# Low-rank mix in plain float32 with V in four bands, and ScalarE copying the second head's transposed exponents in every attention step

## The chip, the cores and the metric

The kernel runs on one core of one Trainium2 chip. The metric is the device time of one execution in microseconds (us). TensorE is called PE, VectorE DVE, ScalarE ACT, GpSimd POOL in the rows; PEld is PE's weight load, SP the engine that issues most DMAs.

## The reference

Three stages follow each other on 2 batches of 768 tokens with 512 features. Everything is float32.

```python
# 1. attention, 8 heads of 64, a window of 96 keys and 8 global keys, ALiBi bias
a = softmax(scale * q @ k.T + bias, masked);  x = a @ v
# 2. low-rank mix over the tokens (rank 32), then a feed-forward network
h = x.transpose(0, 2, 1) @ U @ V              # U [768, 32], V [32, 768]
u = x + h.transpose(0, 2, 1)
x = u + np.maximum(u @ w_ch1, 0.0) @ w_ch2    # 512 -> 2048 -> 512
# 3. real part of a 2-D FFT, normalisation, a second feed-forward network
```

The change is in the low-rank mix between the attention and the first feed-forward network, and in one copy of the attention.

## The kernel before

**Numbers.** The fast matmuls take operands in a rounded form of float32 (`fp32r`, FR in the code). To keep precision the kernel splits a matrix into a rounded part and a remainder (names `wh`/`wo`, `xh`/`xl`, `gh`/`gl`, `vh`/`vl`): ACT casts, then POOL or DVE subtracts, and PE multiplies the parts one after the other. Attention and transposes use plain float32, one matmul per product; such a matmul stands as two records in the trace.

**Attention.** `attn` goes through 8 head pairs `c`, each in 3 steps `j`. In a step PE makes scores (line 484), DVE adds the bias and finds the maximum (492), ACT takes exponents (504), PE transposes them (515) into a `ps_h` bank for each of the two heads `z`, and an engine copies the bank to SBUF as `pt`: ACT at line 517, DVE at line 519. Before the feed-forward network runs (`side_mode` False) the first head always goes to DVE, and the second to ACT for `j` 0 and 1, to DVE for `j` 2. PE then multiplies with V's rows (535), ACT copies (539), and after three steps PE transposes (550) and DVE scales into `xall` (558).

**Low-rank mix.** For each batch `lr_sum` adds U^T x over six token tiles. `us` holds U's rounded part and remainder, each twice, as 128 columns; for every tile and half of the features ACT casts `xh` (337), `xl` is subtracted (338; DVE for batch 0, POOL for batch 1), and PE makes two matmuls of 256 columns (339, 340). Then ACT and DVE make `R` out of the sum (349, 350), and for each tile PE multiplies it with `vh` and `vl` (356, 357), DVE adds into `xall` (358), and some tiles are transposed for the feed-forward network (270, ACT 272, DVE 273).

**Feed-forward.** `ffn` goes through 16 chunks `c` of the hidden size for each block of 512 tokens. In iteration `c` PE makes h(c), 12 matmuls of 512 columns at line 203, and then a(c-1), 12 matmuls at line 225; I use these names below. For chunk `c` ACT casts `wh` (179) and POOL subtracts `wo` in two halves (182); h(c) needs the first half from its third matmul on. In the first block the weights arrive as int64-packed doubles and are decoded two iterations ahead: ACT line 164, DVE lines 166, 168, 170 in that order, the last writing `w`. `wh` and `wo` have three buffers each, so `wh`(c) cannot start before a(c-3) is done.

**Order.** A generator of side work (`drive`) gives one piece after each quarter of an iteration: first the rest of the attention, then batch 1's low-rank mix with the transposes of tiles 6 and 7, then those of tiles 4 and 5. A scheduler sets the final order on each engine; each engine works through its own queue in order. The first block begins at 100.9 us, and batch 1's mix at 158.9 us. PSUM has two `ps_sd` banks; during the first block the attention, `lr_sum` and the transposes of batch 1 share them.

Of the kernel before, what the change touches and what calls it, by code (L numbers as in the profile page):

```python
# [35 lines left out]
class Prog:  # L36
# [252 lines left out]
    def lr_setup(self, pool):  # L289
        nc = self.nc  # L290
        t0, t2, u64, v64 = self.lrt
        ur = t0[:, 2 * NT * RK:]
        for z in range(4):
            self.decode(ur, u64, z)
        yield
        uraw = ur.rearrange("p (t r) -> p t r", t=NT)
        self.us = pool.tile([P, NT, 4 * RK], FR, name="us")
        self.vh = pool.tile([P, S], FR, name="vh")
        self.vl = pool.tile([P, S], FR, name="vl")
        nc.gpsimd.memset(self.vl[2 * RK:P, :].bitcast(F32), 0.0)  # L300
        us = self.us
        for c in (0, 2):
            h, l = us[:, :, c * RK:(c + 1) * RK], us[:, :, (c + 1) * RK:(c + 2) * RK]
            nc.scalar.copy(h, uraw)
            nc.gpsimd.tensor_tensor(l, uraw, h.bitcast(F32), ALU.subtract)
        yield

    def lr_setup2(self, pool):
        nc = self.nc
        t0, t2, u64, v64 = self.lrt  # L310
        vraw = t2[:, 0:S]
        for z in range(4):
            self.decode(vraw, v64, z)
            yield
        nc.scalar.copy(self.vh, vraw)
        nc.gpsimd.tensor_tensor(self.vl[0:2 * RK, :], vraw[0:2 * RK, :], self.vh[0:2 * RK, :].bitcast(F32), ALU.subtract)
        yield

    def w_first(self):
# [4 lines left out]
        self.w_split(0)  # L324
        yield

    def lr_sum(self, b, pool, half):
        nc = self.nc
        if half == 0:
            self.tps = self.psum("m")  # L330
        tps = self.tps
        c = slice(half * 256, half * 256 + 256)
        for t in range(NT):
            x = self.x[b * NT + t]
            xh = pool.tile([P, 256], FR, tag="xh", bufs=2, name=f"xh{b}{t}{half}")
            xl = pool.tile([P, 256], FR, tag="xl", bufs=2, name=f"xl{b}{t}{half}")
            nc.scalar.copy(xh, x[:, c])
            (nc.vector if b == 0 else nc.gpsimd).tensor_tensor(xl, x[:, c], xh.bitcast(F32), ALU.subtract)  # L338
            nc.tensor.matmul(tps[:, c], lhsT=self.us[:, t, :], rhs=xh, start=t == 0, stop=False)
            nc.tensor.matmul(tps[:, c], lhsT=self.us[:, t, :], rhs=xl, start=False, stop=t == NT - 1)  # L340
            yield

    def lr(self, b, pool, halves, tiles):
        nc = self.nc
        for h in halves:
            yield from self.lr_sum(b, pool, h)
        tps = self.tps
        R = pool.tile([P, D], FR, tag="R", bufs=1, name=f"R{b}")
        nc.scalar.copy(R, tps)
        nc.vector.tensor_tensor(R[64:128, :], tps[64:128, :], R[64:128, :].bitcast(F32), ALU.subtract)  # L350
        yield
        for t in range(NT):
            x = self.x[b * NT + t]
            s = slice(t * P, (t + 1) * P)
            hp = self.psum("m")
            nc.tensor.matmul(hp, lhsT=self.vh[:, s], rhs=R, start=True, stop=False)
            nc.tensor.matmul(hp, lhsT=self.vl[:, s], rhs=R, start=False, stop=True)
            nc.vector.tensor_tensor(x, hp, x, ALU.add)
            yield
# [89 lines left out]
    def attn(self, pool, lag1=1, lag2=2):  # L449
# [58 lines left out]
        def s3(u):  # L508
            c, j = U[u]
            pr = st[u]  # L510
            pt = [pool.tile([P, 512], F32, tag="pt", bufs=4, name=f"pt{c}{j}{z}") for z in range(2)]
            for z in range(2):
                tp = self.psum("tr")
                for i in range(4):
                    nc.tensor.transpose(tp[:, i * P:(i + 1) * P], pr[z][:, i * P:(i + 1) * P], self.ident)  # L515
                if self.side_mode or z == 1 and j < 2:
                    nc.scalar.copy(pt[z], tp)  # L517
                else:
                    nc.vector.tensor_copy(pt[z], tp)
            st[u] = pt  # L520
# [300 lines left out]
def arm(tc, pg, fast):  # L821
    with ExitStack() as ctx2:
# [4 lines left out]
        if fast:  # L827
# [14 lines left out]
            pg.w_load(2)  # L842
            while pg.heads < 4:
                step(att, 1)
            for _ in pg.lr_sum(0, pool, 0):
                step(att, 1)
            for _ in chain(pg.lr_setup2(pool), pg.w_first()):
                step(att, 1)
# [2 lines left out]
        else:  # L851
# [161 lines left out]
```

## Time and profile before

| | |
|---|---|
| median of 3 runs | 716.91 us (716.83 to 717.27) |
| the profiled execution | 717.96 us, of which the span of the instructions is 716.2 us |
| PE busy | 694.5 us, 97% of the span |
| DVE, ACT, POOL busy | 51%, 41%, 43% |
| mean granted PE clock | 0.986 |

A busy share is an average over stages. PE's is so high that the few places where PE waits, or runs at a lower granted clock, are what there is to look for; the page's second part, busy tenths in 40 slices, puts them at 60 to 70 us and 160 to 200 us.

### The profile page before, as it was taken

The page shows a single profiled execution, that of the slowest core. Times are in us where ns is not written, and L with a number is a line of the kernel's source. Part 1 is how long each engine was busy: PE and PEld are TensorE (multiplying, and loading weights), DVE is VectorE, ACT ScalarE, POOL GpSimd, SP SyncE. Part 2 cuts the span into 40 slices and gives each one's busy share as a digit, 9 for nine tenths or more (in the row PEclk, how much of TensorE's full clock was granted, in tenths as well). Part 3 has the DMA queues.
Part 4 walks back from the last instruction along what each step waited for, and adds up shares of the span by engine and source line. Part 5 has one row for each costly group of instructions (what it writes and reads, how often), then busy time and mean ns, then how long its engine had stood idle before and what let it go on. Part 6 is the DMA issues. An engine that isn't in the chain of part 4 may idle for free.

```text
span 716.2 us, 9707 instructions
## 1 busy us (share of the span) xinstructions
PE 694.5 (97%) x3584; PEld 569.0 (79%) x3584; DVE 362.4 (51%) x722; ACT 296.3 (41%) x551; POOL 307.5 (43%) x258
## 2 busy tenths in 40 slices
PE   9998999996899999999999999999999999999995
PEld 8776777775678888888888888888888888888884
DVE  4779797655386754348737888124832111211112
ACT  3776666644243444334433334222233333332320
POOL 3104103237456655545534574424454444454450
PEclk9999999998799999999999999999999999999999
DMA  8846618554548877666656442221233223332301
GB/s 258 294 169 208 226 65 256 176 175 149 169 135 298 266 247 255 233 238 211 232 196 213 147 177 89 88 83 66 74 118 133 88 89 113 121 120 97 108 31 64
DMA packets 34393, 115.93 MB, mean 162 GB/s; under 512 B 4128, under 2 KB 4640, under 8 KB 32032
## 3 DMA queue, kind: packets, MB, share of 16 engines
q1 hardware_dynamic: 33024, 111.63, 46.0%
q0 software_dynamic: 1312, 3.59, 1.6%
q8 instruction: 30, 0.49, 0.3%
q14 instruction: 27, 0.22, 0.1%
HBM read 95.27 MB, written 19.92 MB: 161 GB/s over the span
## 4 chain that ended last, share of the span: by engine, by line
PE 90%; DVE 3%; issue 2%; POOL 2%; ACT 1%; DMA 0%; SPq 0%; DVEq 0%; POOLq 0%; ACTq 0%
PE ps_acc L225 35%; PE ps_h L203 35%; PE ps_sd L535 4%; PE ps_acc L484 3%; PE ps_h L515 2%; PE wu L80 2%; PE ps_sd L270 1%; PE ps_sd L484 1%; PE ps_sd L732 1%; POOL wo L182 1%; POOL xl L338 1%; PE ps_sd L746 1%; PE ps_sd L515 1%; PE ps_sd L708 1%; PE ps_sd L759 1%
## 5 line engine op out<-in xcount | busy, mean ns | idle before, releaser
L182 POOL TENSOR_TENSOR wo<-w,wh 128x512 fp32r<-128x512 f32 x192 | 266.6, 1409 | 288.7 <-ACT wh L179 285.3
L203 PE MATMUL ps_h<-uT,wh 128*128 128x512 f32 x768 | 239.9, 393 | 0.0
L211 DVE SCALAR_TENSOR_TENSOR gl<-ps_h,gh 128x512 fp32r<-128x512 f32 x96 | 65.9, 686 | 226.8 <-ACT gh L210 226.7
L179 ACT CAST wh<-w 128x1024 fp32r<-128x1024 f32 x96 | 101.0, 1052 | 172.5 <-PE ps_acc L225 139.8
L203 PEld LDWEIGHTS ps_h<-uT,wh 128*128 128x128 f32 x768 | 141.5, 188 | 29.5 <-issue 2.0
L225 PE MATMUL ps_acc<-wh,gh 128*128 128x512 f32 x384 | 153.4, 400 | 0.0
L225 PE MATMUL ps_acc<-wo,gh 128*128 128x512 f32 x384 | 151.8, 395 | 0.0
L225 PE MATMUL ps_acc<-wh,gl 128*128 128x512 f32 x384 | 151.7, 395 | 0.0
L203 PE MATMUL ps_h<-uT,wo 128*128 128x512 f32 x384 | 150.0, 391 | 0.0
L210 ACT ACTIVATE gh<-ps_h 128x512 fp32r<-128x512 f32 x96 | 57.5, 599 | 148.1 <-PE ps_h L203 148.1
L225 PEld LDWEIGHTS ps_acc<-wh,gl 128*128 128x128 f32 x384 | 73.4, 191 | 15.8
L225 PEld LDWEIGHTS ps_acc<-wh,gh 128*128 128x128 f32 x384 | 73.5, 191 | 14.7 <-issue 0.7
L225 PEld LDWEIGHTS ps_acc<-wo,gh 128*128 128x128 f32 x384 | 73.5, 191 | 14.2
L203 PEld LDWEIGHTS ps_h<-uT,wo 128*128 128x128 f32 x384 | 72.1, 188 | 15.4
L168 DVE SCALAR_TENSOR_TENSOR wr<-wr 128x1024 int32<-128x1024 int32 x32 | 47.9, 1498 | 32.5 <-ACT wr L164 31.2
L504 ACT ACTIVATE T<-T,m 128x256 f32<-128x256 f32 (+1 forms) x96 | 47.8, 499 | 28.2 <-DVE m L492 27.9
L164 ACT ACTIVATE wr<-wr 128x1024 f32<-128x1024 f32 x32 | 36.7, 1147 | 0.0
L535 PE MATMUL ps_sd<-pt,vb 128*64 128x128 f32 x384 | 35.3, 287 | 0.4 <-ACT pt L517 0.4
L492 DVE CUSTOM_DVE_ANT_0 T<-ps_acc,dist 128x256 f32<-128x256 f32 (+1 forms) x76 | 28.4, 418 | 11.0 <-PE ps_acc L484 7.0
L535 PEld LDWEIGHTS ps_sd<-pt,vb 128*64 128x64 f32 x384 | 26.0, 139 | 8.2 <-issue 5.2
L170 DVE SCALAR_TENSOR_TENSOR w<-wr 128x1024 int32<-128x1024 int32 x16 | 24.8, 1548 | 0.6
L437 POOL TENSOR_SCALAR q<-q 128x768 f32<-128x768 f32 x4 | 4.4, 1097 | 47.7 <-PE ps_sd L535 22.9
(171 smaller groups left out, 626.5 us busy)
## 6 DMA issues: line engine op xcount, KB each, us to landing
w<-wscr SPq DMA_DIRECT2D x80, 512.0 KB, 3.3
wr<-wl SPq DMA_DIRECT2D x17, 1024.0 KB, 5.9
wr<-wl SPq DMA_DIRECT2D x60, 256.0 KB, 5.3
wscr<-w SPq DMA_DIRECT2D x16, 512.0 KB, 6.7
wscr<-wd SPq DMA_DIRECT2D x16, 512.0 KB, 2.8
vb<-vw SPq DMA_DIRECT2D x8, 768.0 KB, 5.9
k<-qkg SPq DMA_DIRECT2D x4, 704.0 KB, 7.2
out<-qkt SPq DMA_DIRECT2D x11, 256.0 KB, 3.3
```

Source lines behind the costliest of these rows:

```text
L164: nc.scalar.activation(hi.bitcast(F32), hi.bitcast(F32), AF.Copy, scale=2.0 ** -112))
L168: nc.vector.scalar_tensor_tensor(lo, hi, 3, lo, ALU.logical_shift_left, ALU.bitwise_or)
L179: nc.scalar.copy(hi, raw)
L182: nc.gpsimd.tensor_tensor(lo[:, h], raw[:, h], hi[:, h].bitcast(F32), ALU.subtract)
L203: nc.tensor.matmul(hp, lhsT=w[:, s], rhs=u[:, dd, :], start=n == 0, stop=n == 11)
L210: nc.scalar.activation(gh, hp, AF.Relu)
L211: nc.vector.scalar_tensor_tensor(gl, hp, 0.0, gh.bitcast(F32), ALU.max, ALU.subtract)
L225: nc.tensor.matmul(acc[t], lhsT=g[:, s], rhs=w[:, D:2 * D], start=pf == 0 and m == 0, stop=pf == NF - 1 and m == 2)
L484: nc.tensor.matmul(sp[z][:, o:o + n], lhsT=q[ROWS[z], ts], rhs=win(k[ROWS[z]], t), start=True, stop=True)
L492: nc.vector.tensor_tensor_reduce(out=T[z][:, s], in0=sp[z][:, s], in1=self.dist[z][:, dcol[t]:dcol[t] + width[t]], op0=ALU.add, op1=ALU.mi ...
L504: nc.scalar.activation(T[z][:, s], T[z][:, s], AF.Exp, bias=m[z][:, i:i + 1], scale=-1.0, accum_out=st["s", c, z][:, j, i:i + 1])
L535: nc.tensor.matmul(pv[y * HD:(y + 1) * HD, z * P:(z + 1) * P], lhsT=v[:, vc, d], rhs=pt[z][:, o:o + P], start=i == 0, stop=i == n - 1)
```

## The change

`us` becomes U itself, four times side by side, in plain float32, written by one POOL instruction. `lr_sum` takes x as it is: `xh`, `xl` and their casts and subtractions are gone, and one plain float32 matmul takes the place of two rounded ones. Batch 0 keeps its two halves of 256 columns; batch 1 does all 512 columns at once, in 6 pieces instead of 12. `vh` gets four bands of 32 rows (V rounded, remainder, rounded, remainder) and `vl` is gone, so that one matmul a tile gives the mix; its two bands of remainders are two POOL subtractions of 32 rows instead of one of 64, and POOL's clearing of `vl` is gone. ACT copies the second head's transposed exponents for `j` 2 too. From the low-rank sum on, lines stand 6 or 7 lower in the new file.

```diff
-        self.us = pool.tile([P, NT, 4 * RK], FR, name="us")
-        self.vh = pool.tile([P, S], FR, name="vh")
-        self.vl = pool.tile([P, S], FR, name="vl")
-        nc.gpsimd.memset(self.vl[2 * RK:P, :].bitcast(F32), 0.0)
-        us = self.us
-        for c in (0, 2):
-            h, l = us[:, :, c * RK:(c + 1) * RK], us[:, :, (c + 1) * RK:(c + 2) * RK]
-            nc.scalar.copy(h, uraw)
-            nc.gpsimd.tensor_tensor(l, uraw, h.bitcast(F32), ALU.subtract)
+        self.us = pool.tile([P, NT, 4 * RK], F32, name="us")
+        rep = bass.AP(uraw.tensor, uraw.offset, [list(uraw.ap[0]), list(uraw.ap[1]), [0, 4], list(uraw.ap[2])])
+        nc.gpsimd.tensor_scalar(self.us.rearrange("p t (z r) -> p t z r", z=4), rep, 1.0, 1.0, ALU.mult, ALU.mult)
...
+        self.vh = pool.tile([P, S], FR, name="vh")
         nc.scalar.copy(self.vh, vraw)
-        nc.gpsimd.tensor_tensor(self.vl[0:2 * RK, :], vraw[0:2 * RK, :], self.vh[0:2 * RK, :].bitcast(F32), ALU.subtract)
+        for z in (1, 3):
+            r = slice(z * RK, (z + 1) * RK)
+            nc.gpsimd.tensor_tensor(self.vh[r, :], vraw[r, :], self.vh[r, :].bitcast(F32), ALU.subtract)
...
-        c = slice(half * 256, half * 256 + 256)
+        c = slice(0, D) if half is None else slice(half * 256, half * 256 + 256)
         for t in range(NT):
-            x = self.x[b * NT + t]
-            xh = pool.tile([P, 256], FR, tag="xh", bufs=2, name=f"xh{b}{t}{half}")
-            xl = pool.tile([P, 256], FR, tag="xl", bufs=2, name=f"xl{b}{t}{half}")
-            nc.scalar.copy(xh, x[:, c])
-            (nc.vector if b == 0 else nc.gpsimd).tensor_tensor(xl, x[:, c], xh.bitcast(F32), ALU.subtract)
-            nc.tensor.matmul(tps[:, c], lhsT=self.us[:, t, :], rhs=xh, start=t == 0, stop=False)
-            nc.tensor.matmul(tps[:, c], lhsT=self.us[:, t, :], rhs=xl, start=False, stop=t == NT - 1)
+            nc.tensor.matmul(tps[:, c], lhsT=self.us[:, t, :], rhs=self.x[b * NT + t][:, c],
+                             start=t == 0, stop=t == NT - 1)
             yield
...
-            nc.tensor.matmul(hp, lhsT=self.vh[:, s], rhs=R, start=True, stop=False)
-            nc.tensor.matmul(hp, lhsT=self.vl[:, s], rhs=R, start=False, stop=True)
+            nc.tensor.matmul(hp, lhsT=self.vh[:, s], rhs=R, start=True, stop=True)
...
-                if self.side_mode or z == 1 and j < 2:
+                if self.side_mode or z == 1:
                     nc.scalar.copy(pt[z], tp)
                 else:
                     nc.vector.tensor_copy(pt[z], tp)
...
-        drive(main, 64, chain(att, pg.lr(1, pool, (0, 1), range(6, 8)), pg.tr_gen(0, range(4, 6), pg.x)), 1.0)
+        drive(main, 64, chain(att, pg.lr(1, pool, (None,), range(6, 8)), pg.tr_gen(0, range(4, 6), pg.x)), 1.0)
```

**First place: PE and POOL in h(7), batch 1's sum.** PE before, from the sixth matmul of h(7) on; xh and xl are the parts of x, us is U:

```order
L203 MATMUL ps_h<-uT_1146,wo_1800 128x512
L339 MATMUL ps_sd<-xh_1893,us 128x256
L340 MATMUL ps_sd<-xl_1894,us 128x256
L203 MATMUL ps_h<-uT_1146,wh_1799 128x512
L203 MATMUL ps_h<-uT_1147,wh_1799 128x512
L203 MATMUL ps_h<-uT_1146,wo_1800 128x512
L203 MATMUL ps_h<-uT_1146,wh_1799 128x512
L203 MATMUL ps_h<-uT_1147,wh_1799 128x512
L203 MATMUL ps_h<-uT_1146,wo_1800 128x512
L339 MATMUL ps_sd<-xh_1910,us 128x256
L340 MATMUL ps_sd<-xl_1911,us 128x256
L225 MATMUL ps_acc<-wh_1708,gh_1830 128x512
```

PE of the change at the same place (line 333 is the new matmul):

```order
L203 MATMUL ps_h<-uT_1080,wo_1730 128x512
L333 MATMUL ps_sd<-xall_171,us 128x512
L203 MATMUL ps_h<-uT_1080,wh_1729 128x512
L203 MATMUL ps_h<-uT_1081,wh_1729 128x512
L203 MATMUL ps_h<-uT_1080,wo_1730 128x512
L203 MATMUL ps_h<-uT_1080,wh_1729 128x512
L203 MATMUL ps_h<-uT_1081,wh_1729 128x512
L203 MATMUL ps_h<-uT_1080,wo_1730 128x512
L333 MATMUL ps_sd<-xall_171,us 128x512
L225 MATMUL ps_acc<-wh_1638,gh_1760 128x512
```

Each pair that needed `xl` is now one matmul of 512 columns that needs only `xall`, and the sum is complete at the end of a(6) instead of the end of h(9).

POOL before, from the subtractions of chunk 7's `wo` on:

```order
L182 TENSOR_TENSOR wo_1800<-w_1713,wh_1799 128x512 x2
L338 TENSOR_TENSOR xl_1894<-xall_171,xh_1893 128x256
L182 TENSOR_TENSOR wo_1879<-w_1804,wh_1878 128x512 x2
L338 TENSOR_TENSOR xl_1911<-xall_171,xh_1910 128x256
L338 TENSOR_TENSOR xl_1927<-xall_171,xh_1926 128x256
L338 TENSOR_TENSOR xl_1939<-xall_171,xh_1938 128x256
L338 TENSOR_TENSOR xl_1960<-xall_171,xh_1959 128x256
L182 TENSOR_TENSOR wo_1945<-w_1883,wh_1944 128x512 x2
L338 TENSOR_TENSOR xl_1977<-xall_171,xh_1976 128x256
```

POOL of the change, from the same chunk on:

```order
L182 TENSOR_TENSOR wo_1730<-w_1643,wh_1729 128x512 x2
L182 TENSOR_TENSOR wo_1799<-w_1734,wh_1798 128x512 x2
L182 TENSOR_TENSOR wo_1845<-w_1803,wh_1844 128x512 x2
L182 TENSOR_TENSOR wo_1905<-w_1849,wh_1904 128x512 x2
L182 TENSOR_TENSOR wo_1963<-w_1909,wh_1962 128x512 x2
```

The subtractions of `xl` between those of `wo` are gone; nothing stands in POOL's queue between two chunks.

**Second place: DVE and PE where R is made.** DVE of the change, around iteration 8 (line 344 is R's subtraction, 351 the addition into x):

```order
L170 SCALAR_TENSOR_TENSOR w_1803<-wr_1611 128x1024
L166 TENSOR_SCALAR wr_1696<-wr_1696 128x1024
L211 SCALAR_TENSOR_TENSOR gl_1821<-ps_h,gh_1820 128x512
L168 SCALAR_TENSOR_TENSOR wr_1696<-wr_1696 128x1024
L344 TENSOR_TENSOR R_1859<-ps_sd,R_1859 64x512
L170 SCALAR_TENSOR_TENSOR w_1849<-wr_1696 128x1024
L211 SCALAR_TENSOR_TENSOR gl_1869<-ps_h,gh_1868 128x512
L351 TENSOR_TENSOR xall_171<-ps_sd,xall_171 128x512 x2
L273 TENSOR_TENSOR uT_1896<-ps_sd,uT_1895 128x4x128
```

PE of the change, from the last matmuls of h(8) into a(7) (line 350 multiplies R):

```order
L203 MATMUL ps_h<-uT_1080,wh_1798 128x512
L203 MATMUL ps_h<-uT_1081,wh_1798 128x512
L203 MATMUL ps_h<-uT_1080,wo_1799 128x512
L225 MATMUL ps_acc<-wh_1729,gh_1820 128x512
L225 MATMUL ps_acc<-wo_1730,gh_1820 128x512
L350 MATMUL ps_sd<-R_1859,vh 128x512
L225 MATMUL ps_acc<-wh_1729,gl_1821 128x512
L225 MATMUL ps_acc<-wh_1729,gh_1820 128x512
L225 MATMUL ps_acc<-wo_1730,gh_1820 128x512
L225 MATMUL ps_acc<-wh_1729,gl_1821 128x512
L350 MATMUL ps_sd<-R_1859,vh 128x512
```

Before, R's subtraction stood behind a whole chunk's decode and its first user at the end of a(8). Now R is behind line 168 of chunk 10, and its first user only two matmuls into a(7).

## Rows read from the trace of the kernel before

**Rows 1.** the page, part 1: busy time, share of the span, instructions
```profile
PE 694.5 (97%) x3584; PEld 569.0 (79%) x3584; DVE 362.4 (51%) x722; ACT 296.3 (41%) x551; POOL 307.5 (43%) x258
```

**Rows 2.** TensorE timeline 158.6 to 167.2: start, us, instruction, [idle before <-releaser]
```profile
158.93 0.28 PE L339 MATMUL ps_sd<-xh,us 128*128 128x256 f32 x1
159.04 0.28 PE L340 MATMUL ps_sd<-xl,us 128*128 128x256 f32 x1
159.16 0.39 PE L225 MATMUL ps_acc<-wh,gh 128*128 128x512 f32 x1
...
163.72 0.28 PE L339 MATMUL ps_sd<-xh,us 128*128 128x256 f32 x1
167.08 0.57 PE L340 MATMUL ps_sd<-xl,us 128*128 128x256 f32 x1 [3.08 <-POOL xl L338]
```

**Rows 3.** GpSimd timeline, around the first of these waits, same columns
```profile
161.84 3.50 POOL L182 TENSOR_TENSOR wo<-w,wh 128x512 fp32r<-128x512 f32 x2 [1.37 <-PE ps_h L203]
165.31 3.61 POOL L338 TENSOR_TENSOR xl<-xall,xh 128x256 fp32r<-128x256 f32 x3
```

**Rows 4.** who waited for whom, 0 to 215: us in total, times, longest
```profile
PE ps_sd L340 <- POOL xl L338: 9.2, 3, 3.1
```

**Rows 5.** stretches: us, busy of PE, PEld, DVE, ACT, POOL, granted clock, DMA
```profile
160.00:170.00 10.00, 6.92 (x28) 5.49 (x27) 4.70 (x4) 3.69 (x6) 7.55 (x6) 0.86 0.61 195
...
180.00:190.00 10.00, 7.80 (x29) 6.12 (x28) 3.27 (x2) 3.40 (x5) 5.41 (x5) 0.79 0.39 142
```

**Rows 6.** stretches in which the granted clock was at half, same columns
```profile
64.70:68.10 3.40, 3.40 (x22) 2.41 (x21) 3.40 (x8) 1.13 (x3) 2.79 (x2) 0.50 1.01 251
167.10:170.50 3.40, 3.40 (x10) 2.82 (x11) 0.54 (x1) 0.37 (x1) 1.82 (x2) 0.50 0.88 207
177.40:184.20 6.80, 5.75 (x15) 4.69 (x16) 1.60 (x3) 0.81 (x2) 3.63 (x4) 0.50 0.74 231
191.00:194.40 3.40, 3.40 (x9) 2.73 (x10) 0.69 (x1) 0.58 (x1) 0.00 (x0) 0.50 0.89 214
```

**Rows 7.** chain that ended last, 155 to 260: start, us, what
```profile
157.69 1.40 PE ps_acc L225 x6
...
210.75 0.44 PE ps_sd L270 x4
...
217.12 2.72 PE ps_h L203 x12
...
228.00 2.72 PE ps_h L203 x12
```

**Rows 8.** TensorE timeline 10 to 19: plain float32 warm-up matmuls
```profile
11.11 1.16 PE L80 MATMUL wu<-ident 128*128 128x128 f32 x8
```

**Rows 9.** lines 337 and 519: ns min/median/max, first and last start
```profile
L337 ACT CAST xh<-xall x24: 388/405/421, 42.9 to 186.5; 128x256 fp32r<-128x256 f32 x24
...
L519 DVE COPY pt<-ps_h x24: 674/682/690, 14.9 to 100.4; 128x512 f32<-128x512 f32 x24
```

**Rows 10.** VectorE, TensorE and GpSimd timelines around 61 to 69
```profile
61.34 2.39 DVE L170 SCALAR_TENSOR_TENSOR w<-wr 128x1024 int32<-128x1024 int32 x1
...
64.48 0.86 PE L515 MATMUL ps_h<-ident,T 128*128 128x128 f32 x4 [1.67 <-DVE pt L519]
...
68.88 0.46 PE L484 MATMUL ps_acc<-k,q 64*128 64x128 f32 x2
...
60.82 1.83 POOL L316 TENSOR_TENSOR vl<-lrt,vh 64x768 fp32r<-64x768 f32 x1
```

**Rows 11.** ScalarE and VectorE timelines, decode of chunk 15
```profile
218.42 1.06 ACT L179 CAST wh<-w 128x1024 fp32r<-128x1024 f32 x1 [3.32 <-DVE w L170]
219.38 1.14 ACT L164 ACTIVATE wr<-wr 128x1024 f32<-128x1024 f32 x1
...
220.55 2.85 DVE L168 SCALAR_TENSOR_TENSOR wr<-wr 128x1024 int32<-128x1024 int32 x1 [0.35 <-ACT wr L164]
...
223.93 1.21 DVE L170 SCALAR_TENSOR_TENSOR w<-wr 128x1024 int32<-128x1024 int32 x1
```

More of the change, by code (lines that the diff above doesn't have):

```diff
@@ L325, in w_first, with lr_sum @@
         yield
-    def lr_sum(self, b, pool, half):
+    def lr_sum(self, b, half):
         nc = self.nc
-        if half == 0:
+        if not half:
             self.tps = self.psum("m")
         tps = self.tps
-        c = slice(half * 256, half * 256 + 256)
+        c = slice(0, D) if half is None else slice(half * 256, half * 256 + 256)
         for t in range(NT):
-            x = self.x[b * NT + t]
-            xh = pool.tile([P, 256], FR, tag="xh", bufs=2, name=f"xh{b}{t}{half}")
-            xl = pool.tile([P, 256], FR, tag="xl", bufs=2, name=f"xl{b}{t}{half}")
-            nc.scalar.copy(xh, x[:, c])
-            (nc.vector if b == 0 else nc.gpsimd).tensor_tensor(xl, x[:, c], xh.bitcast(F32), ALU.subtract)
-            nc.tensor.matmul(tps[:, c], lhsT=self.us[:, t, :], rhs=xh, start=t == 0, stop=False)
-            nc.tensor.matmul(tps[:, c], lhsT=self.us[:, t, :], rhs=xl, start=False, stop=t == NT - 1)
+            nc.tensor.matmul(tps[:, c], lhsT=self.us[:, t, :], rhs=self.x[b * NT + t][:, c],
+                             start=t == 0, stop=t == NT - 1)
             yield
@@ L345, in lr @@
         for h in halves:
-            yield from self.lr_sum(b, pool, h)
+            yield from self.lr_sum(b, h)
         tps = self.tps
@@ L844, in arm @@
                 step(att, 1)
-            for _ in pg.lr_sum(0, pool, 0):
+            for _ in pg.lr_sum(0, 0):
                 step(att, 1)
@@ L859, in arm @@
             pg.attn_any(pool)
-            drain(pg.lr_sum(0, pool, 0))
+            drain(pg.lr_sum(0, 0))
             att = None
```

## Prediction

> **What bounds the kernel now.** I read the page first, then its clock and wait views, then timelines. PE is busy 694.5 us of a span of 716.2 us [rows 1], so almost everywhere PE's own instructions set the end, and time can come only from less PE work, from places where PE waits, or from places where its granted clock is low. The table of stretches shows where these are: between 160 and 190 us PE is busy only 6.9 to 7.8 us of each 10, at a granted clock of 0.79 to 0.86 [rows 5]. The list of waits names the cause: three times PE stood at the second matmul of a pair in `lr_sum` until POOL had subtracted `xl`, 9.2 us together [rows 4]. The PE timeline shows the first of them: line 339 starts at 163.72, line 340 only at 167.08, with 3.08 us idle [rows 2]. POOL's timeline shows why: `xl` was queued behind the two halves of the next chunk's `wo`, 3.50 us, and itself took over 1 us [rows 3]. Each wait has an echo: the granted clock falls to its lower level (0.50, 1.2 of 2.4 GHz) for 3.4, 6.8 and 3.4 us [rows 6], right after or around the waits; PE was busy 12.55 us in them, half of which, 6.3 us, it would not have needed at the upper level.
>
> The chain of waits gives this as one number. From the start of a(5) at 157.69 to that of h(15) at 228.00 [rows 7] pass 70.3 us. In between lie 9 groups a and 8 groups h; at full speed a group of 12 matmuls takes 2.72 us [rows 7], 0.227 a matmul, so 17 x 2.72 = 46.2. Batch 1's mix adds 24 matmuls of 256 columns at 0.115 (from 158.93 over 159.04 to 159.16 [rows 2]) = 2.8, 12 of 512 columns = 2.7, and 4 transposes of a tile at 0.44 [rows 7] = 1.8. That is 53.5 us of work in 70.3: 16.8 us are lost, and 9.2 + 6.3 = 15.5 of them are the waits and the low clock just named.
>
> **The change, part by part.**
>
> *PE work.* Plain float32 is dearer. The warm-up matmuls show it: 4 matmuls of 128 columns stand as 8 records in 1.16 us [rows 8], the last record 0.275 long, so 0.126 apart and 0.25 us a matmul. A matmul of 256 columns is not shown for full 128 rows; I take its moving columns as the cost and scale, a little under twice, 0.43 us, and 0.86 us for 512. Bounds: not below the 0.23 of the pair that it replaces, not above 0.50 and 1.0 (twice and four times the row). Batch 0: 12 x (0.43 - 0.23) = +2.4. Batch 1: 6 x 0.86 - 2.8 = +2.4. The 12 matmuls with `vl` go: -2.7. Sum +2.1 us (from -2.7 to +4.0).
>
> *Batch 1's sum.* Its operands are now `xall` alone, done before the sum begins, so the three waits on `xl` and their echoes have no cause left. Work from a(5) to h(15) becomes 46.2 + 5.2 (six new matmuls) + 1.4 (six with `vh`) + 1.8 = 54.6 us. If PE never waited, 70.3 - 54.6 = 15.7 us would come back.
>
> *What is late next.* I laid the new order out by hand with durations from rows. From 157.69 on, a(5), h(7) and a(6) carry two pieces of the sum each and take 2.72 + 2 x 0.86 = 4.44: a(6) ends near 171.0. Only then `wh`(9) gets its buffer, and ACT casts R behind `wh`(9) and the decode of chunk 10 (1.06 + 1.14 [rows 11]), from 173.2 on. DVE's half of R stands behind line 168 of chunk 10, which also starts at 173.2. Line 168 lies between 1.21 (line 170, the same form) and 2.85 [rows 11]; I take 1.8, as POOL works on `wo`(9) at that time. With 0.7 for R itself and the handovers, R is ready near 175.9. PE wants it two matmuls into a(7), at 171.0 + 2.72 + 0.45 = 174.2. So PE waits about 1.7 us there, and by the same layout about 0.6 more at the first transposes, which need a `ps_sd` bank and x from DVE. Below, the first wait is nothing if ACT comes to R early; above, I bound it by the old 3.08 [rows 2].
>
> *The decode.* For each chunk ACT's `wh`(c+1) and line 164, then DVE's 168 and 170, then `wh`(c+2) form a loop. Before, chunk 15 took it from 218.42 to 225.1, 6.7 us, with line 168 at 2.85 [rows 11]; with 168 at 1.8 it would be 5.7. PE's iteration takes 5.44, and 6.3 to 8.9 while the mix runs in it. In my layout `wh` comes 1.1, 1.5 and 1.8 us after PE has begun the iteration in which it is cast, for chunks 13 to 15, and then decoding is over; `wh` may be 5.44 + 0.45 - 1.06 - 1.75 = 3.1 late before PE notices, since h(c) wants only the first half of `wo`, and from its third matmul on (3.50 / 2 = 1.75 us [rows 3]). So it costs nothing, with over 1 us to spare. With the two waits of 1.7 and 0.6 us, h(15) comes 15.7 - 2.3 = 13.4 us earlier, near 214.6.
>
> *Batch 0 and the attention.* There the sum adds +2.4 and the missing `vl` takes 1.4: +1.0 for PE. ACT loses 12 casts of 0.4 us, and DVE 12 subtractions and some copies of 0.68 [rows 9], of which ACT gets the copies. DVE was full around 61 to 72: PE waited 1.67 us for a `pt` copy behind a line 170 of 2.39, and ran at the low clock for 3.4 us after it [rows 10, 6]. The copy that PE wants first is the first head's, which stays on DVE, so I take that wait as staying, and allow 0.5 us for shorter waits after it. POOL's remainder of V takes two instructions of 32 rows instead of one of 64 rows and 768 columns, 1.83 [rows 10]; `wo`'s 128 rows and 512 columns take 1.75, so columns count rather than rows, and two take about 3.7. They stand before the scaling of a q. Before, POOL was done with both at 62.65; 1.83 later would be near 64.5, and the first scores of that q start at 68.88 [rows 10]: these 4 us cover it, and without them up to 1.8 would show. The copy of U on POOL takes the place of longer work there, and several attention steps pass before it is read. Net +0.5 us (from -2 to +3). All that follows the first block is PE at full speed and only moves with it.
>
> POOL and DVE slow each other: line 170 takes 1.21 with POOL idle [rows 11] and 2.39 with POOL at work [rows 10]. If V's second subtraction held DVE up for its whole 1.83, the wait at 64.48 would grow by that, and the low clock after it by a further 1.7 at most: 3.5 us less gain. I take it as hidden, since DVE's work there is not all on the path, and keep 3.5 as a rival. The Trainium skill, SBUF — State Buffer, section "Who interferes with whom", has the rule for this: a VectorE instruction with two inputs in SBUF and a GpSimd one that reads SBUF shut each other out for a whole instruction; by it the sum would come out near 707.6. The doubled line 170 agrees with it; no row shows a subtraction of 32 rows there.
>
> **Sum.** 717.96 (the profiled execution) - 13.4 + 0.5 = 705.1. The median of the runs is 1.05 lower than the profiled execution, so I predict 704.0 us.
>
> **The rivals.**
> - *Clean:* R comes in time, and PE does not wait in the first block. For it: ACT no longer carries the casts of x. Against: my layout, in which R waits for the decode. 15.7 instead of 13.4 and up to 2.5 in the attention: 698.5 to 701.5.
> - *The decode or the clock takes back:* line 168 stays near 2.85 and the loop at 6.7, `wh` falls 1.3 us a chunk behind PE's 5.44 and PE waits in chunks 13 to 15; or R's wait brings the low clock back (a wait of 1.67 did at 64.48), 3.4 us at half, 1.7 lost each time. 707 to 713.
> - *V's remainder holds DVE:* 3.5 lost in the attention, 707.5. For it: DVE has no idle time around 61. Against: DVE's own queue there is shorter by a copy.
> - *Slower:* the waits of PE were only first seen at `xl`, and the true limit is the decode of a chunk. Before, h(7) to h(15) took 70.3 less a(5) and its two pairs, 67.1 us, 8.4 a chunk. If the loop alone needed more than 8.4, nothing would come back and the dearer float32 would stay: 716.9 + 2.1, about 719 (up to 721). Against it: chunk 15 took 6.7 with its worst line 168, and POOL has no `xl` left. It decides only from 8.4 on.
> - *No change:* the gain just eaten, a narrow strip between the two.
>
> **How the numbers follow.** Forecast (701.5 to 707) 0.50, clean 0.22, decode or clock 0.15, V's remainder 0.06, no change 0.02, slower 0.05. The range from 699 to 710 leaves out the lower end of the clean case, the upper half of the decode case, no change and slower, about 0.2; the forecast's own range is 701.5 to 707. About 0.2% (1.4 us) is what a measurement of this kernel can tell from no change: faster than that 0.93, within 0.02, slower 0.05.
>
> **What would show it.** Right: no PE wait on POOL between 158 and 200; h(15) near 214 to 215; a PE wait of 1 to 2 us at line 350 before DVE's R; six pairs of records of line 333 about 0.43 apart in batch 1; the granted clock at the upper level from about 180 on. Wrong: PE waiting for `wo` or `wh` in chunks 9 to 15, `wh` later than 3.1 us into its iteration, records of line 333 more than 0.5 apart, or h(0) later than 104 instead of near 101.4.

## The result, and the profile after

The changed kernel takes 699.27 us (median of 4 runs, 698.70 to 700.11) where the kernel before, run beside it, takes 717.09 (716.83 to 717.50). The ratio is 0.9752, with a 95% interval of 0.9735 to 0.9769. The profiled execution took 699.44 us, with a span of 697.7. The forecast was 704.0 (699.0 to 710.0), so the time lies at the lower edge of the range, where the prediction had put its clean rival, and below the 701.5 to 707 that it gave the forecast itself.

Three marks, each the start of the first matmul of a group in the TensorE timeline (the chain's entries in [rows 7] lie about 0.2 us later), show where the time came from:

| | before | after | less |
|---|---|---|---|
| h(0), start of the first block | 100.88 | 97.17 | 3.7 |
| a(5) | 157.45 | 152.87 | 4.6 |
| h(15) | 227.84 | 209.41 | 18.4 |
| end of the span | 716.2 | 697.7 | 18.5 |
| a(5) to h(15) | 70.39 | 56.54 | 13.85 |

Of the 18.5 us, 13.85 lie between a(5) and h(15), where the prediction had 13.4. The other 4.6 lie ahead of a(5), where it had a loss of 0.5; some 0.5 of the 4.6 is only where the two traces begin, as the experiments show. From h(15) to the end nothing changed (488.3 and 488.2 us).

The stretches after, with the same columns as [rows 5] (busy time of PE, PEld, DVE, ACT, POOL, granted clock, DMA):

```profile
60.00:70.00 10.00, 8.31 (x66) 6.61 (x65) 10.00 (x30) 9.40 (x28) 7.58 (x5) 1.00 0.67 219
160.00:170.00 10.00, 10.00 (x39) 7.04 (x38) 5.74 (x6) 3.15 (x4) 4.56 (x3) 1.00 0.51 157
180.00:190.00 10.00, 10.00 (x49) 8.15 (x48) 8.98 (x13) 5.90 (x7) 5.03 (x3) 1.00 0.65 175
```

Against [rows 5], PE is busy for all of 160 to 170 and 180 to 190, and the clock is at its upper level. It stays there until 695 us, so all four half-clock stretches of [rows 6] are gone. The first row is the one to remember: between 60 and 70 us DVE has no idle time at all.

Who waited for whom from 20 to 215 us, for PE (us in total, times, longest):

```profile
PE ps_h L508 <- DVE pt L512: 0.9, 1, 0.9
PE ps_h L508 <- ACT pt L510: 0.8, 1, 0.8
PE ps_sd L333 <- DVE xall L551: 0.4, 1, 0.4
PE ps_h L543 <- ACT pt L510: 0.4, 1, 0.4
PE ps_sd L350 <- DVE R L344: 0.2, 1, 0.2
```

The line on `xl` of [rows 4], 9.2 us, has no successor. The new waits in the first block are two of 0.4 and 0.2 us: the first piece of batch 1's sum comes before x is written, and R comes a little late.

The TensorE timeline there:

```profile
155.18 1.12 PE L333 MATMUL ps_sd<-xall,us 128*128 128x512 f32 x2 [0.44 <-DVE xall L551]
...
157.28 1.02 PE L333 MATMUL ps_sd<-xall,us 128*128 128x512 f32 x2
157.74 1.02 PE L203 MATMUL ps_h<-uT,wh 128*128 128x512 f32 x2
158.60 0.40 PE L203 MATMUL ps_h<-uT,wo 128*128 128x512 f32 x1
...
170.73 0.50 PE L350 MATMUL ps_sd<-R,vh 128*128 128x512 f32 x1 [0.25 <-DVE R L344]
```

From 157.28 to 158.60 PE does one plain float32 matmul of 512 columns and two fast ones of 0.227: 1.32 - 0.45 = 0.87 us for the new one, against the 0.86 that the prediction scaled from the warm-up.

### The profile page after: what moved, and what is told of

The parts are those of the page before. It is cut to its first block, busy times and chain, and to the rows that moved or that the text cites. A ratio compares the mean times of both kernels' runs of the same rounds, so it can differ in the third digit from the quotient of the medians.

```text
span 697.7 us, 9578 instructions
## 1 busy us (share of the span) xinstructions
PE 685.6 (98%) x3560; PEld 559.9 (80%) x3560; DVE 352.9 (51%) x704; ACT 290.0 (42%) x531; POOL 296.8 (43%) x245
## 4 chain that ended last, share of the span: by engine, by line
PE 90%; DVE 4%; ACT 2%; DMA 1%; issue 1%; POOL 0%; SPq 0%; DVEq 0%; POOLq 0%
PE ps_acc L225 35%; PE ps_h L203 35%; PE ps_sd L528 4%; PE ps_acc L477 2%; PE ps_h L508 2%; PE wu L80 2%; PE ps_sd L270 1%; DVE wr L168 1%; DMA wr<-wl 1%; PE ps_sd L477 1%; PE ps_acc L333 1%; PE ps_sd L725 1%; PE ps_sd L739 1%; PE ps_sd L508 1%; PE ps_sd L701 1%
## 5 line engine op out<-in xcount | busy, mean ns | idle before, releaser
L203 PEld LDWEIGHTS ps_h<-uT,wo 128*128 128x128 f32 x384 | 72.1, 188 | 15.7 <-issue 0.2
L528 PE MATMUL ps_sd<-pt,vb 128*64 128x128 f32 x384 | 32.8, 282 | 0.0
L166 DVE TENSOR_SCALAR wr<-wr 128x1024 int32<-128x1024 int32 x32 | 22.8, 713 | 0.0
## 6 DMA issues: line engine op xcount, KB each, us to landing
k<-qkg SPq DMA_DIRECT2D x4, 704.0 KB, 7.1
```

What stands on the lines that cost most here:

```text
L203: nc.tensor.matmul(hp, lhsT=w[:, s], rhs=u[:, dd, :], start=n == 0, stop=n == 11)
L528: nc.tensor.matmul(pv[y * HD:(y + 1) * HD, z * P:(z + 1) * P], lhsT=v[:, vc, d], rhs=pt[z][:, o:o + P], start=i == 0, stop=i == n - 1)
```

## The experiments

The origin of a trace moves: the fourth attention step's first bias instruction on DVE lies between 19.9 and 21.3 us, before any edit takes effect. In the table h(0) and a(5) are shifted so that it lies at 20.36 in all, as in the changed kernel. The "head pair" is the fifth pair of heads, from its first bias instruction to that of the next pair, three attention steps.

| kernel | median us | h(0) | a(5) | head pair | a(5) to h(15) |
|---|---|---|---|---|---|
| before | 717.1 | 100.35 | 156.92 | 13.30 | 70.39 |
| changed | 699.3 | 97.17 | 152.86 | 10.86 | 56.54 |
| before, xl on DVE | 707.0 | 100.31 | 157.44 | 13.28 | 59.14 |
| changed, batch 0 in parts | 703.5 | 101.70 | 157.43 | 14.20 | 56.55 |
| changed, batch 1 in parts | 711.2 | 97.51 | 153.19 | 10.85 | 66.69 |
| changed, without the copy | 702.1 | 98.62 | 155.35 | 13.11 | 56.53 |
| before, no remainder of V | 713.4 | 98.53 | 155.13 | 11.84 | 70.50 |
| before, the copy alone | 714.8 | 99.69 | 155.41 | 12.25 | 67.54 |
| changed, without the bands | 700.8 | 97.17 | 152.89 | 10.61 | 57.94 |
| changed, V's remainder after q | 700.9 | 98.81 | 154.54 | 13.11 | 56.48 |
| changed, batch 1 in parts ahead | 701.0 | 97.51 | 153.73 | 10.84 | 57.54 |
| changed, decode later | 695.8 | 94.05 | 149.75 | 10.84 | 56.50 |
| changed, decode between | 695.8 | 94.06 | 149.75 | 12.05 | 56.49 |
| the same, batch 1 in parts ahead | 698.5 | 94.36 | 150.56 | 12.07 | 57.57 |

In these runs the kernel before had medians of 716.07 to 716.55 with single times from 711.44 to 718.71, and a mean granted clock of 0.994 in the fastest and 0.986 to 0.989 near 718. The traces that keep the waits on `xl` do not agree in how long the clock is low in batch 1's sum: 13.6 us in [rows 6], two stretches of about 3.4 with the same 9.2 us of waits in the kernel with the copy alone. The kernels whose PE does not wait there spread over 0.6 to 2.3 us, those with these waits over 3.6 to 7.3, though in more executions. So differences under 3 us between kernels that keep these waits are read from the marks, not from the medians.

The head pair before and after, with the columns of [rows 5]:

```profile
59.96:73.27 13.31, 10.62 (x79) 8.17 (x77) 13.31 (x36) 9.54 (x28) 7.46 (x6) 0.87 0.63 181
59.49:70.35 10.86, 9.17 (x71) 7.32 (x70) 10.86 (x34) 9.93 (x29) 8.44 (x6) 1.00 0.65 218
```

DVE has no idle time in either; PE has 2.7 and 1.7 us of it.

### The first block: is it POOL's queue or float32?

```diff
-            (nc.vector if b == 0 else nc.gpsimd).tensor_tensor(xl, x[:, c], xh.bitcast(F32), ALU.subtract)
+            nc.vector.tensor_tensor(xl, x[:, c], xh.bitcast(F32), ALU.subtract)
```

> The kernel before, with one edit: batch 1's xl is subtracted on DVE instead of POOL, so it no longer stands behind wo. Theory (the queue on POOL was the cause, and float32 is only one way out of it): PE's three waits on POOL at the second matmul of a pair (9.2 us) and the low clock after them (6.3 us) go; PE's work stays as before; DVE gets 12 subtractions of about 0.5 us more among its decode lines, so small waits of 1 to 3 us in all may come: 717.1 - 15.5 + 1 to 3, that is 702.5 to 705. Rival (float32 itself is needed, because xl on DVE stands behind lines 168 and 170 of the decode and holds them up in turn): PE waits as long on DVE as it did on POOL, 712 or more.

It took 707.04 us (705.27 to 707.49), ratio 0.9865 (0.9813 to 0.9916). PE's waits on `xl`:

```profile
PE ps_sd L340 <- DVE xl L338: 3.8, 3, 1.3
```

The wait for `xl` fell from 9.2 to 3.8 us, and the clock stayed at its upper level through the block. a(5) to h(15) fell from 70.39 to 59.14, which is 11.25 of the 13.85 us. So the place in POOL's queue was the cause, and float32 is one cure of it. The time lies between the two theories' ranges: the theory allowed 1 to 3 us of new waits, and there were 3.8. The difference to the changed kernel adds up: 56.54 - 0.7 (its two small waits) + 3.8 + 0.5 (this kernel's two other waits in the block) + 1.4 (six `vl` matmuls) - 2.4 (pairs cheaper than float32) = 59.1.

The other way round, the changed kernel gets batch 1's old sum back, with `xl` on POOL and a second `us` in two parts:

```diff
+            if b == 1:
...
+                nc.scalar.copy(xh, x[:, c])
+                (nc.vector if b == 0 else nc.gpsimd).tensor_tensor(xl, x[:, c], xh.bitcast(F32), ALU.subtract)
+                nc.tensor.matmul(tps[:, c], lhsT=self.us2[:, t, :], rhs=xh, start=t == 0, stop=False)
+                nc.tensor.matmul(tps[:, c], lhsT=self.us2[:, t, :], rhs=xl, start=False, stop=t == NT - 1)
```

> The changed kernel, with batch 1's sum in two rounded parts as before (xl on POOL, 12 pieces of 256 columns). Theory (the 13.8 us between a(5) and h(15) come from xl leaving POOL's queue and from the clock that fell after the waits): PE waits on POOL's xl at three places again, the clock falls after them, h(0) stays near 97.2, time 711 to 714. Rival (part of that gain comes from one matmul with vh instead of two, from ACT's and DVE's lighter load, or from an earlier start of the block): 703 to 709.

It took 711.2 us (709.64 to 713.69, 10 runs). h(0) moved by 0.3 us, and PE waited again:

```profile
PE ps_sd L345 <- POOL xl L343: 9.1, 3, 3.1
```

Two half-clock stretches of about 3.4 us came back, where [rows 6] has 13.6 us of them in this block:

```profile
164.50:167.80 3.30, 3.30 (x10) 2.64 (x9) 0.00 (x0) 0.41 (x1) 1.79 (x3) 0.50 0.78 261
174.70:178.00 3.30, 2.90 (x7) 2.37 (x8) 0.95 (x2) 0.41 (x1) 2.25 (x3) 0.50 0.78 174
```

PE was busy 6.2 us in the two, half of it lost: 9.1 of waits and 3.1 of low clock, less 2.4 of cheaper matmuls, are 9.8 us; a(5) to h(15) grew by 10.15. The theory holds, at the lower end of its range.

Then the parts were made early enough on DVE, two pieces ahead of the matmuls that read them (`x_parts` casts `xh` and subtracts `xl`, and is called twice before the sum begins):

```diff
+                xh, xl = self.xparts.pop(0)
+                nc.tensor.matmul(tps[:, c], lhsT=self.us2[:, t, :], rhs=xh, start=t == 0, stop=False)
+                nc.tensor.matmul(tps[:, c], lhsT=self.us2[:, t, :], rhs=xl, start=False, stop=t == NT - 1)
+                self.x_parts(pool)
```

> The changed kernel, but batch 1's sum in two rounded parts again, with xh cast and xl subtracted on DVE two pieces ahead of the matmuls that read them. PE's work falls by 6 x 0.86 - 12 x 0.23 = 2.4 us against plain float32; DVE gets 12 subtractions of some 0.5 us and ACT 12 casts of 0.4 in the first block. Theory (plain float32 only served to take xl out of POOL's queue; made early enough on DVE, the cheaper parts need no wait): no wait on xl, 697 to 698.3. Rival (on DVE xl and the decode hold each other up, as with xl on DVE without the lead, where PE waited 3.8 us): 699.5 to 703.

It took 701.03 us (699.33 to 701.68), so the rival was right. PE still waited 2.7 us for `xl`, four times, and 0.54 for R, while DVE in turn waited 2.0 us for ACT's casts. These 3.2 us are 2.5 more than the changed kernel's two waits, so they alone spend the 2.4 us of cheaper matmuls; a(5) to h(15) is 1.0 us longer, and for the rest of that no wait is listed. Of the ways tried, plain float32, dearer on PE, is the cheapest for the block; it needs no parts from another engine.

### The attention: which edit gave the 4 us?

Each edit was taken out of the changed kernel by itself. First batch 0's sum, back in two parts (the code as above with `b == 0` and DVE):

> The changed kernel, with batch 0's sum in two rounded parts as before (ACT casts xh, DVE subtracts xl, pairs of matmuls). Theory 1 (the attention stage gained because ACT and DVE lost these casts and subtractions): h(0) comes 2 to 4 us later than the 97.2 of the changed kernel, time 701.5 to 703.5. Rival (the gain there comes from the ACT copy, the four bands or the shorter stall at 63 us): PE saves 12 x 0.2 = 2.4 us of float32 work and nothing else changes, h(0) 0 to 2.4 us earlier, 697 to 699.3.

703.49 us (702.53 to 704.81); h(0) comes 4.5 us later. The price was at the top of theory 1's range and the mark beyond it; but 3.3 of the 4.5 us lie inside the head pair, where no cast or subtraction of x stands. Then the copy:

```diff
-                if self.side_mode or z == 1:
+                if self.side_mode or z == 1 and j < 2:
```

> The changed kernel without its copy edit: for j 2 the second head's pt goes to DVE again. Theory 2 (the attention stage gained 3.7 us up to h(0) because ACT took a copy of 0.68 us from DVE in each of eight head pairs): the wait for a pt copy near 63 us goes back to about 1.7 us with the low clock after it, h(0) near 100, time 702 to 703.5. Rival (the copy moves work that was hidden on DVE): h(0) within 0.7 us of 97.2, time 698.7 to 700.

702.08 us (701.84 to 702.47): the price of theory 2, but not its place. The wait for the first head's copy stayed at 0.9 us; PE waited 1.34 us for the maximum that DVE makes of the scores instead. The head pair grew by 2.25 us; h(0) came 1.5 and a(5) 2.5 us later.

The bands (in this kernel V counts twice, since the four bands of `us` are now alike; its instructions are those of the edit):

```diff
-            nc.tensor.matmul(hp, lhsT=self.vh[:, s], rhs=R, start=True, stop=True)
+            nc.tensor.matmul(hp, lhsT=self.vh[:, s], rhs=R, start=True, stop=False)
+            nc.tensor.matmul(hp, lhsT=self.vl[:, s], rhs=R, start=False, stop=True)
```

> The changed kernel with vl kept: two matmuls a tile for the mix, one POOL subtraction of 64 rows instead of two of 32. PE's work grows by 12 x 0.227 = 2.7 us. Theory (the bands are worth PE's work in the first block, 6 x 0.227 = 1.4, and cost something in the attention, where two subtractions keep POOL and DVE in each other's way for 4.6 instead of 1.8 us): 1.4 to 2.7 slower by PE's work, 0 to 1 back at 57 to 63 us: 699.7 to 702. Rival (the bands' longer work on POOL costs nothing): 702 to 702.2. Second rival (it costs more than PE's work gains): below 699.3.

700.75 us (699.56 to 701.70), within the theory's range. In the first block the six matmuls cost 57.94 - 56.54 = 1.40 us, the 1.4 of the prediction; h(0) did not move at all: the head pair was 0.25 shorter without the second subtraction on POOL, and batch 0's six matmuls, which stand between 83 and 92 us, took back 0.3, not 1.4. PE reads busy there almost all the time (26.73 of 26.82 us from the head pair's end to h(0) in the changed kernel), so why they cost so little stays open.

What is left is the remainder of V. The kernel before without its subtraction:

```diff
-        nc.gpsimd.memset(self.vl[2 * RK:P, :].bitcast(F32), 0.0)
+        nc.gpsimd.memset(self.vl.bitcast(F32), 0.0)
...
-        nc.gpsimd.tensor_tensor(self.vl[0:2 * RK, :], vraw[0:2 * RK, :], self.vh[0:2 * RK, :].bitcast(F32), ALU.subtract)
```

> The kernel before, leaving out one instruction: POOL's subtraction that fills vl (1.83 us at 60.82). vl is cleared whole instead, so the remainder of V is left out of the sum. Theory (between 60 and 74 us DVE is the bound, and POOL's work beside it makes its lines 168 and 170 longer): line 170 at 61.34 falls from 2.39 to about 1.25, PE's wait for the pt copy at 64.48 from 1.67 to about 0.5, and h(0) comes 1 to 1.5 us earlier than 100.9; nothing changes in the first block, so the time falls by 1 to 1.5 us, or by up to 3 if the low clock at 64.7 goes with the wait. Rival (that wait is not on the path, as other DVE or ACT work ends last): h(0) within 0.4 us of before.

713.37 us, ratio 0.996 (0.994 to 0.998). The VectorE and TensorE timelines there:

```profile
61.51 1.22 DVE L170 SCALAR_TENSOR_TENSOR w<-wr 128x1024 int32<-128x1024 int32 x1
...
63.47 0.63 PE L514 MATMUL ps_h<-ident,T 128*128 128x128 f32 x4 [0.70 <-DVE pt L518]
```

Line 170 fell from 2.39 [rows 10] to 1.22 and PE's wait from 1.67 to 0.70, and h(0) came 1.8 us earlier, as did a(5). The half clock near 64.7 did not come either (1.00 from 60 to 70 us). So one POOL instruction of 1.83 us was worth 1.8 us, its share of the low clock included.

The copy alone on the kernel before:

> The kernel before with the copy edit alone (ACT copies the second head's pt for j 2 too). Theory (DVE is the bound between 60 and 74 us, so each copy of about 0.6 us taken from it there comes back, as the run without the copy edit showed with 2.7 us at a(5)): h(0) 0.6 to 2.7 us earlier than 100.9, time 0.6 to 2.7 us below before. Rival (the copy pays only when ACT has lost the casts of x and DVE the subtractions; with them ACT is as late as DVE was): h(0) within 0.5 us of before or later, time as before or up to 1 us above.

714.83 us, ratio 0.9982 (0.9962 to 1.0002), not told from no change by the times; h(0) came 0.7 and a(5) 1.5 us earlier, so the marks speak for the theory, weakly at h(0). GpSimd, VectorE and TensorE show a reason for so little:

```profile
60.79 1.83 POOL L316 TENSOR_TENSOR vl<-lrt,vh 64x768 fp32r<-64x768 f32 x1
...
60.85 2.86 DVE L170 SCALAR_TENSOR_TENSOR w<-wr 128x1024 int32<-128x1024 int32 x1
...
64.45 0.63 PE L515 MATMUL ps_h<-ident,T 128*128 128x128 f32 x4 [2.14 <-DVE pt L519]
```

Line 170 began 0.06 us after POOL's subtraction instead of 0.52 [rows 10], met more of it, and took 2.86 us. It ended at 63.71, 1.1 us after the subtraction; in the kernel before it ended at 63.73, also 1.1 us after it, so starting earlier gained nothing. This fits a copy that pays in full (2.5 us at a(5) in the changed kernel) only where the remainder of V is out of the way, but it is not shown: the casts of x, which the rival blames, stand in this kernel too, and no two runs with and without the copy have only one of the two.

In the changed kernel the remainder is out of the way, because the scheduler put it there: on POOL the subtractions stand ahead of the scaling of the third q, not behind it as before. VectorE and GpSimd of the changed kernel:

```profile
57.62 1.95 DVE L168 SCALAR_TENSOR_TENSOR wr<-wr 128x1024 int32<-128x1024 int32 x1 [0.17 <-ACT wr L164]
59.49 0.28 DVE L485 CUSTOM_DVE_ANT_0 T<-ps_acc,dist 128x128 f32<-128x128 f32 x1
60.87 1.47 DVE L170 SCALAR_TENSOR_TENSOR w<-wr 128x1024 int32<-128x1024 int32 x1
...
70.35 0.28 DVE L485 CUSTOM_DVE_ANT_0 T<-ps_acc,dist 128x128 f32<-128x128 f32 x1
...
56.67 4.59 POOL L314 TENSOR_TENSOR vh<-lrt,vh 32x768 fp32r<-32x768 f32 x2 [22.36 <-ACT vh L311]
61.35 1.68 POOL L430 TENSOR_SCALAR q<-q 128x768 f32<-128x768 f32 x1
```

(59.49 and 70.35 are the two ends of the head pair.) The subtractions run beside line 168 (1.95 us, and 1.22 in the kernel before), ahead of the full stretch and 4 us earlier than in [rows 10], and are done 0.4 us into line 170. One kernel moves them back behind q (`v_rest` issues the two) and leaves the order on PE, DVE and ACT as it is:

```diff
-            for _ in chain(pg.lr_setup2(pool), pg.w_first()):
+            for i, _ in enumerate(chain(pg.lr_setup2(pool), pg.w_first())):
                 step(att, 1)
+                if i == 4 + 3:
+                    pg.v_rest()
```

> The changed kernel with one move on POOL: the two subtractions of V's remainder stand behind the scaling of the third q instead of ahead of it, as they do where batch 0's sum is in two parts. The order on PE, DVE and ACT is the same as in the changed kernel. Theory (much of the attention stage's gain lies in where V's remainder falls beside DVE's lines 166, 168 and 170): the subtractions start near 60.8 instead of 56.67, line 170 at 61 takes about 2.4 instead of 1.47 and line 166 behind it 1.7 instead of 0.71, PE's wait for the pt copy near 63 us grows from 0.90 to about 1.7, and h(0) comes 2 to 3.5 us later than 97.2: 701 to 703. Rival (the gain comes from the casts and subtractions of x that are gone): h(0) within 0.7 us of 97.2, 698.7 to 700.

700.85 us (700.52 to 702.60), ratio 0.9797 (0.9782 to 0.9813), which lies wholly above the changed kernel's interval. Its GpSimd, VectorE and TensorE timelines:

```profile
58.50 1.92 POOL L434 TENSOR_SCALAR q<-q 128x768 f32<-128x768 f32 x1 [23.43 <-ACT wr L164]
60.50 4.59 POOL L319 TENSOR_TENSOR vh<-lrt,vh 32x768 fp32r<-32x768 f32 x2
...
61.01 2.41 DVE L170 SCALAR_TENSOR_TENSOR w<-wr 128x1024 int32<-128x1024 int32 x1
...
63.94 1.70 DVE L166 TENSOR_SCALAR wr<-wr 128x1024 int32<-128x1024 int32 x1
...
64.16 0.63 PE L512 MATMUL ps_h<-ident,T 128*128 128x128 f32 x4 [1.66 <-ACT pt L514]
```

and one of its stretches, with the columns of [rows 5]:

```profile
65.20:68.50 3.30, 3.12 (x19) 2.39 (x20) 3.30 (x9) 1.00 (x4) 3.28 (x2) 0.50 0.85 282
```

Line 170 at 2.41, line 166 at 1.70 and PE's wait of 1.66 came as expected, and the half clock at 65 with them; only the sum was smaller, 1.6 us at h(0) and 1.7 at a(5) instead of 2 to 3.5. So about 1.7 of the 4.1 us that the shifted marks show ahead of a(5) hang on where this one POOL operation falls, and on nothing that the change computes. It also explains batch 0's sum in parts: there POOL has q first again (its subtractions start at 60.79), and some 2.9 of that kernel's 4.6 us at a(5) are left for the sum itself, for the place of DVE's line 168 and for the low clock near 72. These three were not parted further. Taken out singly, batch 0's new sum is worth 4.6 us at a(5), the copy 2.5 and V's place 1.7, together far more than the 4.1 gained: they act on the same full stretch, and their shares do not add.

### Taking DVE's load out of the full stretch

If DVE bounds 60 to 70, other work there can go too. The decode of weight chunks 0 and 1, which PE wants only at h(0), was moved behind the attention of batch 0:

```diff
-            for _ in chain(pg.lr_setup2(pool), pg.w_first()):
+            for _ in pg.lr_setup2(pool):
                 step(att, 1)
             while pg.heads < 8:
                 step(att, 1)
+            wf = pg.w_first()
...
             if att is not None:
                 step(att, 1)
+                step(wf, 1)
```

> The changed kernel with one move: the decode of weight chunks 0 and 1 (six DVE instructions of 0.7 to 2 us, two on ACT, two on POOL) no longer stands between 55 and 72 us, where DVE is busy all the time, but beside the second half of batch 0's sum and the mix, from about 75 us on, where DVE was busy 1.97 and 2.96 of 5 us. Theory (DVE is what bounds 60 to 74 us): PE's waits of 0.90 and 0.80 us there go, h(0) comes 1 to 2.5 us earlier than 97.2, time 697 to 698.5. Rival (DVE then holds up the later attention steps or wh(0) comes late for h(0)): h(0) at 97.2 or later, time 699 to 702.

695.78 us (695.50 to 696.73), ratio 0.9721 (0.9686 to 0.9757), better than expected. h(0) and a(5) come 3.1 us earlier than in the changed kernel. The interval of its ratio overlaps the changed kernel's, but the single times, 695.50 to 696.73 and 698.70 to 700.11, do not. The head pair itself stayed at 10.84 us:

```profile
58.56:69.40 10.84, 10.84 (x106) 8.46 (x104) 7.96 (x34) 9.56 (x31) 3.79 (x3) 1.00 0.46 156
```

DVE is no longer full there, and PE is: it got through 106 matmul records where the changed kernel has 71, and the pairs ahead of it and behind it shortened instead, from 14.96 to 12.82 and from 18.83 to 17.61 us. The TensorE timeline shows what is late next:

```profile
78.38 1.53 PE L528 MATMUL ps_sd<-pt,vb 128*64 128x128 f32 x16 [0.84 <-ACT R L343]
80.68 0.73 PE L350 MATMUL ps_acc<-R,vh 128*128 128x512 f32 x2 [0.77 <-DVE R L344]
...
94.30 0.66 PE L508 MATMUL ps_h<-ident,T 128*128 128x128 f32 x4 [1.14 <-DVE uT L273]
```

Chunk 1's decode now stands around R. Chunk 0's part was brought forward into DVE's gaps to clear that place:

```diff
             while pg.heads < 8:
                 step(att, 1)
+                i += 1
+                if 3 < i < 8:
+                    step(wf, 1)
```

> The kernel with the decode of weight chunks 0 and 1 moved later (median 695.8), with chunk 0's part brought forward again into the steps where DVE then had idle time (0.34, 0.86 and 1.15 us between 57 and 66 us), so that chunk 1's part is out of the way when R is made. There PE waited 0.84 us behind R on ACT and 0.77 us for R on DVE, and 1.14 for uT on DVE. Theory: the two waits at R go, 694 to 695.2. Rival (the waits only move to another DVE result): 695.5 to 697.

695.83 us (695.32 to 696.85). The three waits, 2.75 us, are gone, none of PE's listed waits there is longer than 0.4 us, and yet h(0) and a(5) stand where they stood, to 0.01 us. The head pair grew by 1.2 us in return. PE's busy time between the bias mark at 20.36 and h(0) rose from 70.2 to 72.4 us for the same matmuls, so the list of waits is not the whole of what PE loses here; what bounds this last version was not found. With batch 1's parts made ahead as well:

> Both of the above: chunk 0's and chunk 1's decode spread, and batch 1's sum in two rounded parts with xl on DVE two pieces ahead. If the two are independent the time is the spread one's less what the parts gave alone: 692 to 694 if both theories hold, about the spread kernel's time or above it if the parts cost DVE what they save PE.

698.45 us (697.66 to 698.86): the parts cost 2.6 us here and 1.8 on the changed kernel, no help in either. The decode moved later, spread or not, beats both kernels.

## Why the prediction came out as it did

**The first block was right in cause, and near in size.** Predicted 13.4, measured 13.85. The waits on `xl` and the low clock after them went, and came back, at 9.1 and 3.1 us, when only this edit was undone. The price of a float32 matmul (0.86, measured 0.87) and of a mix matmul (1.4 for six, measured 1.40) held. Line 168 in chunks 10 to 15 was laid out at 1.8 us; it took 1.40, 1.72, 1.71, 1.40, 1.38 and 3.11, 1.79 in the mean. `wh`(15) was cast 2.7 us into its iteration instead of 1.8, still inside the 3.1, and PE waited for no weights.

**The wait for R was mis-sized inside it.** Predicted 1.7, measured 0.25. ScalarE and VectorE after:

```profile
168.43 0.57 ACT L343 CAST R<-ps_sd 128x512 fp32r<-128x512 f32 x1
...
168.55 1.40 DVE L168 SCALAR_TENSOR_TENSOR wr<-wr 128x1024 int32<-128x1024 int32 x1 [4.14 <-ACT wr L164]
169.98 0.69 DVE L344 TENSOR_TENSOR R<-ps_sd,R 64x512 fp32r<-64x512 f32 x1
```

Counted from a(5), ACT's cast came at 15.6 us (laid out: 15.5) and R was ready at 17.8 (18.2). PE came to it at 17.6 instead of 16.5, held up by the 0.44 for x and by 0.7 in small steps that were not parted. The loss was 1.9 us (56.54 less 54.6) instead of 2.3, but of another kind: 0.7 of waits, none of it at the transposes where 0.6 was laid out, and 1.2 of PE's time that the sum does not have. That the two come out so close is luck.

**The step that failed is "Net +0.5 us (from -2 to +3)" for batch 0 and the attention.** a(5) came 4.1 us earlier on the shifted marks, 4.6 with the origin, outside its own bounds. Three things were wrong in it.
- It charged PE's work, +1.0 us, as if PE were the bound. It had read that DVE was full around 61 to 72, and did not draw from it that work taken off DVE comes back: the head pair, with DVE busy all the time, fell from 13.30 to 10.86 us. Nor did PE's term show outside that stretch, where PE reads busy almost all the time: batch 0's six more matmuls of the mix moved nothing at h(0), and the matmuls from the bias mark to h(0), the same 608 or 609 records, are 74.6 us of busy time in the changed kernel and 72.4 and 70.2 in the two with the decode moved. PE's busy time there is not the sum of its matmuls' prices; what else fills it is open.
- "The copy that PE wants first is the first head's, which stays on DVE, so I take that wait as staying." The wait halved, with the copy edit and without it, and it was the smaller part: the second head's copy was in DVE's queue ahead of the next maximum, and taking it away was worth 2.25 us in one head pair.
- It priced V's remainder where it stood before. It had read that the new order puts the subtractions ahead of the scaling of q, and asked only what this does to q, not which DVE instructions they would then run beside. The rival in which V's remainder holds DVE named the right mechanism, with the wrong sign for this order: it costs 1.8 us in the kernel before, and 1.7 when the changed kernel is given the old place.

The Trainium skill, SBUF — State Buffer, section "Who interferes with whom", says that a VectorE instruction with two inputs in SBUF and a GpSimd one that reads SBUF shut each other out. The trace agrees, with line 170 at 1.22 without the subtraction and 2.39, 2.41 and 2.86 beside it. What this costs depends on which DVE instruction is met, and the prediction had the wrong one.

The clean rival's time was met, but not by its account: it had 15.7 us in the block and up to 2.5 ahead of it; it was 13.85 and 4.6. Of the forecast's own signs, h(15) near 214 to 215 and a wait of 1 to 2 us for R did not come (209.4 and 0.25); the clock, the spacing of line 333 and the missing waits on POOL did.

## What to carry to other kernels

Before pricing an edit, find for each stretch which engine has no idle time. PE's 97% of the whole span hid a head pair in which DVE was busy 13.31 of 13.31 us and PE 10.62; there work taken from DVE came back, by an edit or by moving it elsewhere. When two versions differ in a queue's order, read that order for the engines off the path too: an operation on POOL that moved by one place was worth 1.7 us here, through the DVE instructions that it ran beside and the low clock that followed. A dearer instruction on PE that needs no parts from another engine can beat cheaper ones that wait in two queues. And gains that act on one full stretch do not add up.

## What the runs showed of the hardware

The granted clock did not follow a single wait. PE waited 1.67 us before the half clock near 64.7 in the kernel before and 1.66 in the kernel with V's remainder after q; a wait of 2.14 us at the same place in the kernel with the copy alone left it at 1.00. In the kernel before, times between 711 and 719 us go with mean clocks from 0.994 down to 0.986.

Two subtractions of 32 rows and 768 columns took POOL 4.59 us in the changed kernel, 2.30 each, and 3.71, or 1.86 each, in the kernel with the decode later, where DVE was busy for 2.85 of the 3.71 us instead of 4.42 of the 4.59; one of 64 rows took 1.83 [rows 10]. So half the rows saved nothing, and cutting it by rows doubled it. Line 166, which reads one tensor, grew from 0.68 in the kernel before to 1.70 beside such a subtraction.
